# Two weight loads cut in two and issued between other casts, in a kernel of windowed attention and a ReGLU feed-forward layer

## The chip, the cores and the metric

The kernel runs on one core of one Trainium2 chip. The metric is the device time of one execution in microseconds, from the first to the last thing that the device does for it; the profile's span, from the first instruction to the last, is somewhat shorter. Times are medians of several executions.

The engines are named as in the profile: PE (matrix multiply; PEld is its weight load), DVE (vector), ACT (activation), POOL (general purpose) and SP (which here only issues transfers). Each takes its instructions in the order in which they stand in its queue; between engines there are semaphores. Transfers run on 16 DMA engines, which all issuing engines share.

## The reference

The inputs are q, k and v of 4 batches, 8 heads, 768 positions and 64 columns, and three weights. Attention is causal, with a window of 128 positions and 4 sink positions that are always seen; its output, 3072 tokens of 512, goes through a feed-forward layer of width 1536. Cut to what matters:

```python
scores = q @ k.T / 8                       # per batch and head
keep = (pos_k < 4) | ((0 <= pos_q - pos_k) & (pos_q - pos_k < 128))
a = softmax(where(keep, scores, -1e9))
x = (a @ v)                                # heads side by side: (3072, 512)
out = (maximum(x @ w_gate, 0) * (x @ w_val)) @ w_out
```

## The kernel before

The attention is cut into 16 **units**, each of two heads of one batch: unit 0 to 3 are batch 0, unit 4 to 7 batch 1, and so on. A unit's k, q and v are loaded as f32 into one of four staging buffers (`stg`), by SP, in the order k, q, then v in two halves, one per head. They are cast to bf16 into `kn`, `qn` and `vn`: for unit 0 by DVE and ACT in part, for all others by POOL (lines 126 and 129; line 130 repeats the four sink rows of v, line 338 casts a batch's last positions of v from `vt`). PE transposes `kn` and `qn` into `kT` and `qT` (line 149), computes the scores (line 181), ACT takes the exponential, DVE multiplies by the mask where that was not added to the scores, and PE multiplies by v and by ones for the sums (line 206). DVE normalises and leaves the unit's part of `xT` (lines 279 to 284).

The feed-forward layer is cut into **chunks** of 128 columns of the width 1536 and half a batch, 384 tokens: four matmuls against `w_gate` (line 294), four against `w_value` (line 300), ReLU on ACT, the product on DVE into `hT`. Its second product, with `w_out` (line 314), follows in pieces of up to three matmuls after each chunk. For batch 0 the chunks run over columns 0 to 383 for both halves of the tokens, six chunks, then over the next 384 columns, and so on. So the first **quarter** of a weight, 384 columns, serves chunks 0 to 5, and the second quarter is first wanted by chunk 6.

The order is written out by hand. The attention is a list of stages, and the table `PLAN` says how many of them are issued before which chunk: 28 before chunk 0. In these are all the stages of units 0 to 3 and the first three of unit 4. The transposes of unit 5 come after chunk 1. At one stage of unit x, `ahead(x)` issues work for later units: SP's loads, POOL's casts of unit x + 3, and POOL's loads of weights.

All weights are loaded by POOL, since these DMAs also cast from f32 to bf16: `load_w` for quarters of `w_gate` and `w_value`, `load_wo` for thirds of `w_out`. Their data goes over one queue, q0 in the profile; what SP issues goes over q1. Before the first stage POOL's order is: the casts of unit 1's k and q, unit 0's v, unit 1's v, unit 2's k and q; the first quarter of `w_gate`; the cast of unit 2's v. Then `ahead(0)` issues the first quarter of `w_value` and the casts of unit 3, and `ahead(1)` the casts of unit 4 and the second quarter of both weights. The casts of unit 5 follow in `ahead(2)`. Loads on SP stand in the order of units and run some units ahead; load k of unit 4 is issued at 15.56 us, its q at 16.42, its v at 17.41 and 18.03.

The functions that the change touches, and the lines that call them:

Of the kernel before, what the change touches and what calls it, by code (L numbers as in the profile page):

```python
# [33 lines left out]
def kernel(  # L34
# [12 lines left out]
    nc = tc.nc  # L47
# [4 lines left out]
    d_model, d_ff = moe_w_gate.shape  # L52
# [25 lines left out]
    wg = const.tile([128, KO, d_ff], BF16, name="wg")  # L78
    wv = const.tile([128, KO, d_ff], BF16, name="wv")
# [139 lines left out]
            nc.tensor.matmul(out=warm_ps[0][:, 0:128], lhsT=ident[:], rhs=ident[:], start=True, stop=True,  # L219
                             skip_group_check=True)  # L220

    def load_w(c, which=(1, 1)):

        n = d_ff // 4
        for w, dst, wanted in ((moe_w_gate, wg, which[0]), (moe_w_val, wv, which[1])):
            if wanted:
                nc.gpsimd.dma_start(out=dst[:, :, c * n:(c + 1) * n],
                                    in_=w.rearrange("(ko ki) n -> ki ko n", ki=128)[:, :, c * n:(c + 1) * n])

    def load_wo(c):  # L230
        nc.gpsimd.dma_start(out=wo[:, 4 * c:4 * c + 4, :],
                            in_=moe_w_out.rearrange("(ko ki) n -> ki ko n", ki=128)[:, 4 * c:4 * c + 4, :])
# [89 lines left out]
    with tc.manual_schedule():  # L322
        U = [Unit(i) for i in range(B * NP)]
        on_array = []

        def at(x):
            return U[x] if 0 <= x < len(U) else None

        def casts(u, what, eng=nc.gpsimd):
            for w in what:  # L330
                u.cast(w, eng)
# [5 lines left out]
        def cast_t(b):  # L337
            nc.gpsimd.tensor_copy(v6[b % 2][0:24, :, :], vt[b % 2][:])

        def load(x):  # L340
            if not U[x].p:
                load_t(U[x].b)
            for f in (lambda e: U[x].load_kq("k", e), lambda e: U[x].load_kq("q", e),
                      lambda e: U[x].load_v(e, 0), lambda e: U[x].load_v(e, 1)):
                f(nc.sync)

        def held(x):

            if x < len(U):
                nc.vector.memset(U[x].stg[0:1, 0:1], 0.0)  # L350
                load(x)
# [24 lines left out]
        cast_t(0)  # L376
        casts(U[1], "v")
        casts(U[2], "kq")
        load_w(0, (1, 0))
        casts(U[2], "v")  # L380
        load(4)

# [3 lines left out]
        def ahead(x):  # L386

            if x == 3:
                load(6)
            elif x == 4:  # L390
                load(7)
            elif x >= 5:
                held(x + 3)
            if 4 <= x < 6:
                for c in ((0,), (1, 2))[x - 4]:
                    load_wo(c)
            if x == 0:
                load_w(0, (0, 1))
            if at(x + 3) is not None:
                casts(at(x + 3), "kqv")  # L400
                if (x + 3) % NP == 0:
                    cast_t((x + 3) // NP)
            if x in (1, 3, 4):
                load_w((0, 1, 1, 2, 3)[x])
            if x == 0:
                load(5)

        def unit_stages(x):
            u, prev, nxt = U[x], at(x - 1), at(x + 1)

            def s(gi):
                def f():
                    if gi == 0 and nxt is not None and nxt.xbar:
                        nxt.X()
                    u.S(gi)
                    if x == 0 and gi < 2:
                        warm(5)
                return f

            def v():  # L420
                if prev is not None:
                    norm(prev, 1, ps_at if on_array else ps_gv)

            def t():
                if nxt is not None:
                    if not nxt.xbar:
                        nxt.T(not on_array)
                    nxt.sinkk()
                ahead(x)

            def v0():
                norm(u, 0, ps_at if on_array else ps_gv)

            if x < NP:
                return [s(0), s(1), v, t, s(2), v0]
            return [s(0), v, s(1), t, s(2), v0]

        def pair_stages(x):
# [26 lines left out]
            first_outs = outs(U[x - 1], 1) if x == 8 else outs(U[x - 1], 0, 1)  # L465
            a = then(scores((u, 0), (u, 1)))
            a_ = then(first_outs, lambda: ahead(x), w.sinkk)
            c = then(scores((u, 2), (w, 0)))
            d = then(outs(u, 0, 1), lambda: ahead(x + 1), lambda: nxt is not None and nxt.sinkk())
            e = scores((w, 1), (w, 2))  # L470
            first = [then(turn(w), a)] if w.xbar else [a, turn(w)]
# [28 lines left out]
        n = S // 2  # L500
        for ci, (b, h, m) in enumerate(ORDER):
# [11 lines left out]
            if count[b, h] == FM:  # L513
                for t in range(3 * h, 3 * h + 3):
                    w = d_model // 2 if (b, t) == (B - 1, 5) else d_model
# [38 lines left out]
```

## Time and profile before

| what | us |
|---|---|
| median of 4 runs (lowest, highest) | 257.73 (257.38, 257.97) |
| the profiled execution | 257.89 |
| its span, first to last instruction | 256.1 |
| PE busy | 247.7 |
| POOL busy | 62.1 |
| chain that ended last: PE's share of the span | 86% |
| the same: DMA's share | 8% |

Only the first 50 us have to do with the change. Of the stretch from 15 to 50 us, by fives (busy time of an engine in each, and the mean busy share of the 16 DMA engines):

| from | PE | DVE | ACT | POOL | DMA |
|---|---|---|---|---|---|
| 15 | 4.67 | 4.66 | 3.89 | 4.68 | 1.18 |
| 20 | 5.00 | 4.52 | 4.51 | 1.95 | 1.19 |
| 25 | 3.67 | 3.42 | 3.62 | 1.70 | 1.17 |
| 30 | 3.62 | 4.83 | 1.99 | 5.00 | 1.02 |
| 35 | 5.00 | 4.05 | 3.52 | 4.75 | 1.22 |
| 40 | 5.00 | 4.44 | 1.88 | 3.69 | 1.28 |
| 45 | 5.00 | 3.26 | 3.79 | 3.49 | 1.26 |

A DMA share above 1 means that packets' times overlap on an engine. Issuing a weight DMA keeps POOL for 0.74 to 0.88 us; a DMA's own time, to its landing, is told apart from that. The weight DMAs of the first quarter are issued at 15.04 (`w_gate`, landing 7.6 us later) and 17.52 (`w_value`, 10.3 us).

### The profile page before, as it was taken

The numbers are of one execution on the slowest core, as the hardware profiler recorded it, in microseconds if no ns is written. First come the engines' busy times: TensorE is split into PE (matmuls) and PEld (weight loads), VectorE is DVE, ScalarE is ACT, GpSimd is POOL, SyncE is SP. The second block draws the span as 40 slices with busy tenths as digits, with TensorE's granted clock in tenths as the row PEclk, the third lists the DMA queues.
The fourth block names the chain that finished last, engine by engine and source line by source line (L and its number), as shares of the span: only waits on it lengthen the run. The fifth ranks groups of instructions, "written<-read, shape, count | busy, mean of one in ns | idle before, by whom it ended". The sixth has DMA issues, their size and how long they took to land.

```text
span 256.1 us, 5232 instructions
## 1 busy us (share of the span) xinstructions
PE 247.7 (97%) x2058; PEld 144.6 (56%) x2058; DVE 148.7 (58%) x313; ACT 117.2 (46%) x190; POOL 62.1 (24%) x94
## 2 busy tenths in 40 slices
PE   7999699999999999999999999999999999999994
PEld 7556455556555565655565655656565555555443
DVE  2598788697956686787587654565575223223100
ACT  2878753736545426452635255152433332333212
POOL 6694597511705041404221300000000000000000
PEclk9999999999999999999999999999999999999999
DMA  7999999999668598859947712211011101111132
GB/s 207 306 269 259 288 242 255 202 252 220 118 129 160 116 176 170 126 109 180 221 109 146 144 41 72 35 41 44 0 41 44 41 0 41 44 41 41 44 123 84
DMA packets 73160, 33.17 MB, mean 130 GB/s; under 512 B 59696, under 2 KB 70192, under 8 KB 73136
## 3 DMA queue, kind: packets, MB, share of 16 engines
q1 hardware_dynamic: 65760, 27.73, 47.2%
q0 software_dynamic: 5808, 4.72, 11.6%
q10 hardware_dynamic: 1568, 0.39, 0.7%
q8 instruction: 16, 0.26, 0.4%
q14 instruction: 8, 0.07, 0.1%
HBM read 28.51 MB, written 6.29 MB: 136 GB/s over the span
## 4 chain that ended last, share of the span: by engine, by line
PE 86%; DMA 8%; DVE 2%; POOL 1%; issue 1%; ACT 0%; DVEq 0%; POOLq 0%; ACTq 0%
PE gp L294 26%; PE op L314 24%; PE vp L300 24%; PE ops L206 7%; PE sps L181 4%; DMA stg<-in_q_dram 4%; DMA vt<-in_v_dram 3%; DMA stg<-in_k_dram 1%; PE tkq L149 1%; POOL qn L126 1%; DVE ee L187 0%; DVE R L282 0%; DVE xT L284 0%; DVE R L279 0%; POOL vn L129 0%
## 5 line engine op out<-in xcount | busy, mean ns | idle before, releaser
L297 ACT ACTIVATE gs<-gp 128x384 f32<-128x384 f32 x96 | 47.4, 493 | 87.3 <-PE gp L294 56.4
L302 DVE TENSOR_TENSOR hT<-gs,vp 128x384 bf16<-128x384 f32 x96 | 52.0, 549 | 49.2 <-PE vp L300 46.9
L300 PE MATMUL vp<-xT,wv 128*128 128x384 bf16 x384 | 78.1, 326 | 1.0 <-DVE R L279 0.9
L294 PE MATMUL gp<-xT,wg 128*128 128x384 bf16 x384 | 78.5, 327 | 0.5 <-DVE xT L284 0.5
L314 PE MATMUL op<-wo,hT 128*128 128x512 bf16 (+1 forms) x300 | 74.4, 371 | 0.0
L300 PEld LDWEIGHTS <-wv 128*128 128x128 bf16 x384 | 37.5, 98 | 26.2 <-issue 1.5
L185 ACT ACTIVATE ee<-sps 128x1006 bf16<-128x1006 f32 (+2 forms) x48 | 44.6, 962 | 16.7 <-PE sps L181 16.4
L294 PEld LDWEIGHTS <-wg 128*128 128x128 bf16 x384 | 34.3, 98 | 29.8 <-issue 3.7
L314 PEld LDWEIGHTS <-hT 128*128 128x128 bf16 x300 | 29.4, 98 | 25.1
L187 DVE TENSOR_TENSOR ee<-ee,msk 128x1006 bf16<-128x1006 bf16 (+2 forms) x36 | 27.9, 776 | 18.3 <-ACT ee L185 18.0
L126 POOL CAST kn<-stg 128x768 bf16<-128x768 f32 x15 | 12.7, 850 | 56.3 <-DVE hT L302 29.8
L318 ACT COPY ot<-op 128x512 f32<-128x512 f32 (+1 forms) x25 | 14.2, 569 | 22.0 <-PE op L314 21.7
L282 DVE STREAM_TRANSPOSE R<-rc 128x384 f32<-128x384 f32 x32 | 18.5, 578 | 1.1
L284 DVE TENSOR_TENSOR xT<-ops,R 128x384 bf16<-128x384 f32 x32 | 17.8, 557 | 1.7
L279 DVE STREAM_TRANSPOSE R<-ops 128x384 f32<-128x384 f32 x24 | 13.9, 579 | 7.9 <-PE ops L206 7.6
L129 POOL CAST vn<-stg 128x768 bf16<-128x768 f32 x16 | 14.0, 875 | 13.7 <-DMA stg<-in_v_dram 9.3
L206 PEld LDWEIGHTS <-ones 128*64 128x64 bf16 x288 | 12.3, 110 | 7.2 <-issue 7.0
L206 PE MATMUL ops<-ee,vn 128*64 128x255 bf16 (+7 forms) x256 | 15.2, 240 | 0.0
L126 POOL CAST qn<-stg 128x768 bf16<-128x768 f32 x15 | 12.5, 831 | 10.6 <-DMA stg<-in_q_dram 10.6
L181 PEld LDWEIGHTS <-kT 64*128 64x128 bf16 x128 | 6.0, 93 | 13.5 <-issue 10.5
L181 PE MATMUL sps<-qT,kT 64*128 64x251 bf16 (+2 forms) x128 | 13.5, 250 | 0.0
L181 PE MATMUL sps<-qT,kTs 64*128 64x248 bf16 (+1 forms) x96 | 11.7, 253 | 0.5 <-DVE kTs L162 0.5
(57 smaller groups left out, 139.6 us busy)
## 6 DMA issues: line engine op xcount, KB each, us to landing
stg<-in_k_dram SPq DMA_DIRECT2D x16, 384.0 KB, 6.6
stg<-in_q_dram SPq DMA_DIRECT2D x16, 384.0 KB, 6.7
out_dram<-ot SPq DMA_DIRECT2D x23, 256.0 KB, 2.0
stg<-in_v_dram SPq DMA_DIRECT2D x30, 192.0 KB, 5.6
wg<-in_moe_w_gate_dram POOLq DMA_DIRECT2D x4, 384.0 KB, 7.2
wv<-in_moe_w_val_dram POOLq DMA_DIRECT2D x4, 384.0 KB, 9.7
wo<-in_moe_w_out_dram POOLq DMA_DIRECT2D x3, 512.0 KB, 12.4
stg<-in_v_dram ACTq DMA_DIRECT2D x2, 192.0 KB, 6.3
```

Of the source, the lines that this page charges most:

```text
L126: cp((self.kn if what == "k" else self.qn)[:], self.staging(what).rearrange("p h (n d) -> p n h d", d=64))
L181: nc.tensor.matmul(out=ps[:, h, c:c + w], lhsT=self.kw(j, r), rhs=qT[s][r, qa:qa + w], start=not self.biased, stop=True, skip_group_check= ...
L185: nc.scalar.activation(x, ps[:, :, 0:c], Act.Exp, bias=0.0, scale=scale)
L187: nc.vector.tensor_tensor(x, x, bc(msk[:, m0:m0 + c], 2), op=Alu.mult)
L206: nc.tensor.matmul(out=ps[1 - what][64 * h:64 * h + 64, qa - q0:qa - q0 + w], lhsT=self.vw(j, h) if what else ones[:], rhs=ee[s][:, gi, h, ...
L282: nc.vector.transpose(r[:, 1, 0:w], bass.AP(a.tensor, a.offset, [a.ap[0], [1, nb], [0, 32]]))
L284: nc.vector.tensor_tensor(xTs[u.b][:, u.p, c0:c0 + w], o[:, 0:w], r[:, 1, 0:w], op=Alu.mult)
L294: nc.tensor.matmul(out=gp[:, 0:n], lhsT=wg[:, ko, m * 128:(m + 1) * 128], rhs=x[:, ko, c0:c0 + n], start=ko == 0, stop=ko == KO - 1)
L297: nc.scalar.activation(gs[:, 0:n], gp[:, 0:n], Act.Relu, bias=0.0, scale=1.0)
L300: nc.tensor.matmul(out=vp[:, 0:n], lhsT=wv[:, ko, m * 128:(m + 1) * 128], rhs=x[:, ko, c0:c0 + n], start=ko == 0, stop=ko == KO - 1)
L302: nc.vector.tensor_tensor(hT[:, m, c0:c0 + n], gs[:, 0:n], vp[:, 0:n], op=Alu.mult)
L314: nc.tensor.matmul(out=op, lhsT=hTs[b][:, m, t * 128:(t + 1) * 128], rhs=wo[:, m, c0:c0 + n], start=m == 0, stop=m == FM - 1)
```

## The change

`load_w` takes the weights that it is to load as letters and a range of blocks of 128 columns within the quarter; without these it loads a whole quarter of both, as before. The first quarter of each weight is now loaded in two parts. The first part, columns 0 to 127, is issued for `w_gate` and then `w_value` between the q cast and the v cast of unit 2 (the third pair of heads). The second part, columns 128 to 383, is issued in `ahead(0)` in turn with the casts of unit 3 (the fourth pair): its k cast, `w_gate`, its q cast, `w_value`, its v cast. So POOL issues 13 weight DMAs in place of 11; the bytes are the same. Each of the new DMAs still has 512 rows to move, one of each of 128 partitions and 4 blocks, of 128 or 256 columns in place of 384. All other loads, and the work of all other engines, stand in the order in which they stood.

```diff
-    def load_w(c, which=(1, 1)):
-
-        n = d_ff // 4
-        for w, dst, wanted in ((moe_w_gate, wg, which[0]), (moe_w_val, wv, which[1])):
-            if wanted:
-                nc.gpsimd.dma_start(out=dst[:, :, c * n:(c + 1) * n],
-                                    in_=w.rearrange("(ko ki) n -> ki ko n", ki=128)[:, :, c * n:(c + 1) * n])
+    def load_w(c, which="gv", m=(0, 3)):
+
+        for x in which:
+            w, dst = (moe_w_gate, wg) if x == "g" else (moe_w_val, wv)
+            a, b = c * 384 + m[0] * 128, c * 384 + m[1] * 128
+            nc.gpsimd.dma_start(out=dst[:, :, a:b], in_=w.rearrange("(ko ki) n -> ki ko n", ki=128)[:, :, a:b])
...
         casts(U[1], "v")
         casts(U[2], "kq")
-        load_w(0, (1, 0))
+        load_w(0, m=(0, 1))
         casts(U[2], "v")
...
             if x == 0:
-                load_w(0, (0, 1))
+                casts(U[3], "k")
+                load_w(0, "g", (1, 3))
+                casts(U[3], "q")
+                load_w(0, "v", (1, 3))
+                casts(U[3], "v")
+            elif at(x + 3) is not None:
+                casts(at(x + 3), "kqv")
             if at(x + 3) is not None:
-                casts(at(x + 3), "kqv")
                 if (x + 3) % NP == 0:
                     cast_t((x + 3) // NP)
```

## The prediction

> **What bounds the kernel now.** I read the busy rows first: PE is busy 97% of the 256.1 us span, so only time that PE loses can be won, and PE cannot absorb a new wait. Then the chain of waits, from 16 us on (start, duration, what; lines left out between):
>
> ```profile
> 16.42 9.17 DMA stg<-in_q_dram
> ...
> 25.71 0.84 POOL qn L126
> ...
> 26.60 0.51 PE tq L149 x6
> ...
> 33.65 0.81 PE vp L300 x4
> 34.46 0.67 PE tkq L149 x12
> ...
> 42.77 0.65 PE vp L300 x4
> ```
>
> The end hangs on unit 4's q load: issued at 16.42, landed at 16.42 + 9.17 = 25.59, cast by POOL, transposed by PE. PE waits 1.3 us for that cast ("PE tq L149 <- POOL qn L126" among its waits); from 33.65 the chain is PE without a break. The change works on POOL and its DMA queue, so POOL's timeline is next (start, duration, instruction, in brackets the idle time before it):
>
> ```profile
> 23.08 0.82 POOL L126 CAST kn<-stg 128x768 bf16<-128x768 f32 x1 [1.89 <-DMA stg<-in_k_dram]
> 25.71 0.83 POOL L126 CAST qn<-stg 128x768 bf16<-128x768 f32 x1 [1.81 <-DMA stg<-in_q_dram]
> 29.07 0.83 POOL L129 CAST vn<-stg 128x768 bf16<-128x768 f32 x1 [2.52 <-DMA stg<-in_v_dram]
> 29.96 0.50 POOL L130 COPY vn<-vn 4x384 bf16<-4x384 bf16 x1
> 30.41 0.61 POOL L338 CAST v<-vt 24x512 bf16<-24x512 f32 x1
> 30.97 0.74 POOL L227 DMA_DIRECT2D wg<-in_moe_w_gate_dram  x1
> 31.71 0.75 POOL L227 DMA_DIRECT2D wv<-in_moe_w_val_dram  x1
> 32.44 0.84 POOL L126 CAST kn<-stg 128x768 bf16<-128x768 f32 x1
> 33.21 0.84 POOL L126 CAST qn<-stg 128x768 bf16<-128x768 f32 x1
> ```
>
> Unit 4's k, q and v casts each wait for a load. Behind the v cast stand the issues of the second quarter of w_gate and w_value, and unit 5's casts. That second quarter lands 10.8 us after 31.71, at 42.5, and the weight loads show who waits:
>
> ```profile
> 42.54 0.49 PEld L300 LDWEIGHTS <-wv 128*128 128x128 bf16 x4 [0.16 <-DMA wv<-in_moe_w_val_dram]
> ```
>
> The weight load waited for w_value and started 0.06 us before its matmul's turn at 42.60. So there is **no slack here**: PE can gain nothing past 42.6 unless this DMA lands earlier, and whatever it lands later than about 42.55 is lost, since PE takes instructions in order and is full afterwards.
>
> **What the DMA engines charge.** Packets and share of 16 engines by queue; stretches 44 to 45 (weights alone), 47.2 to 47.8 (w_out alone), 38 to 39 (weights with k and q), 24 to 24.5 (weights with v) and 41.2 to 41.7 (v nearly alone):
>
> ```profile
> q0 software_dynamic: 274, 0.20, 132.0%
> ...
> q0 software_dynamic: 119, 0.12, 118.7%
> ...
> q0 software_dynamic: 124, 0.09, 59.6%
> q1 hardware_dynamic: 126, 0.18, 59.2%
> ...
> q0 software_dynamic: 87, 0.07, 85.3%
> q1 hardware_dynamic: 82, 0.02, 33.5%
> ...
> q1 hardware_dynamic: 468, 0.12, 109.8%
> q0 software_dynamic: 18, 0.01, 16.7%
> ```
>
> Q0 carries weights, q1 what SP issues. Where both have work they move packets one for one (124 and 126, 87 and 82), whatever their size. Service times per engine: weights alone 16 x 1000/274, about 60 ns with the tiny semaphore packets taken off; k and q 16 x 1000/125 - 60 = 68; v about (16 x 500 - 18 x 60)/468 = 15. A weight and a v packet together take 16 x 500/85 = 94, so mixing costs 94 - 60 - 15, about 18. Each weight DMA is 512 packets, 32 per engine, of 1536 B read and 768 B written.
>
> **The change part by part.**
>
> *POOL.* Two more issues, 2 x 0.75 = 1.5 us. The issue of w_value before unit 2's v cast moves that from 16.18 to about 16.7; unit 3's k cast stays at about 18.1, its q cast goes from 19.02 to 19.6 (ends 20.4, PE reads it at 20.53), its v cast from 19.80 to 21.1. All is done by 22.5, before unit 4's k load lands (the cast starts at 23.08). Cost nothing, hidden by POOL's 1.89 us of idleness; without that cover, unit 4's k cast would be late, but PE takes it only at 24.84. No SP load's staging buffer is released late: the one of unit 6, held by unit 2's v cast, is issued at 28.0. POOL's later DMAs wait for older ones eight back; the last such pair is 7 us apart or more.
>
> *The first FFN chunk.* Its weights landed at 15.04 + 7.6 = 22.7 and 17.52 + 10.3 = 27.8 and are used at 29.9 and 30.9; nobody waited. Having 128 columns sooner is worth **0**. The parts for columns 128 to 383 are used from 32.6 on; issued at about 18.8 and 20.3 and given the 10.3 us of the slowest such row, they are there by 30.6.
>
> *Unit 4's k and q loads.* Per engine 16 packets each, one for one with weight packets. Now those are small: 512 B read, 256 written. If a packet has the fixed part that 15 ns at 256 B and 68 at 1536 give (a line of 0.041 ns per byte and 5 ns), it takes 5 + 55/3 = 23 ns instead of 60. 32 x 37 ns = 1.2 us at most, of which a part is lost because k and q packets only begin near 20 us, when part of the small ones has passed. Estimate: q lands 0.6 to 1.2 earlier, and most of PE's 1.3 us wait at 26.60 goes. That is what can be won, and it does not reach the end: what is late next is unit 4's **v**.
>
> *Unit 4's v load*, second half, issued at 18.03, landing 10.9 later, 28.9. By then all of the quarter has gone through the engines before (27.8), and will have after: v has 96 packets per engine, more than the 64 middle ones it alternates with. So v is late by the whole difference in DMA work: 64 packets at 60 = 3.84 us before; after, 64 at 23 + 64 at 5 + 55 x 2/3 = 42, 4.16 us: +0.3. And the quarter now alternates with v for some 64 packets an engine, where before w_value's last 25 or so did: I take 30 more x 18 ns = +0.5. Sum **+0.9 us** (rounded up for the second small part, which may start after the first is done and leave engines idle near 19.5). Bounds: no cost but for bytes, 0 (a little below if the last part is so late that v passes it); and packets by their recorded duration instead of their service time: 1.32 x 16000/274 = 77 ns at 768 B and 1.187 x 9600/119 = 96 at 1024 B, a line that gives 58 at 512 B and 39 at 256 B, so 64 x (58 + 39 - 77) = 1.3, with the mixing 1.8. I stay nearer the service times, since the engines overlap packets (shares above 100%).
>
> Two rules of the Trainium skill, DMA: Bandwidth & Descriptors, speak against the change. "Anatomy of one DMA" gives each software DMA a fixed 2.0 us; two more would be +4 us. The trace's row is the second quarter's two issues, 0.74 us apart, and what each DMA adds to a full queue is its packets' time; so I count none of it. "Why small descriptors are slow" puts about 3 cycles on each packet beside one per 32 B: 19, 35 and 51 cycles for 512, 1024 and 1536 B read, (19 + 35)/51 = +6% or +0.2 us, against +0.3 by this trace's row; the mixing, which that section does not have, is the larger term.
>
> *What hangs on v.* POOL's v cast from 29.07 to 30.0, the second quarter's issues from 30.97 to 31.9, unit 5's q cast ending at 34.05 + 0.9 = 34.95 where PE wanted it at 34.58: unit 5's transposes end 0.4 late though PE came early. Then w_value's second quarter lands at 42.5 + 0.9 = 43.4, and PE's matmul goes from 42.60 to 43.45: **+0.85 us**, carried to the end. The profiled execution took 257.89 us (256.1 of span), 0.16 over the median; 257.89 + 0.85 = 258.74, against the median 258.6.
>
> **The rivals.** (a) *Packets cost their bytes alone.* V is late by 0 to 0.3; the gain at 26.60 is taken back at 34.58 and 42.54. Against it: the 94 ns row. Time 257.5 to 258.2, no change. (b) *Faster:* q lands 1.2 us earlier and the last part starts so late that v's packets pass it; the second quarter's issue moves forward with v. For it: the first quarter's w_value took 10.3 us where w_gate took 7.6, so software DMAs issued among casts may start late. It decides once v lands more than 0.5 earlier; PE's next bound is its own 1.3 us wait, so 256.5 to 257.2, say 257.1. (c) *Much slower:* packets at their recorded durations, v late by 1.8, and the same at 42.54: 257.7 + 1.75 = 259.5. That the change does not do what it says is excluded for the order of issues on POOL; its small parts may still be served later than issued, which is (b).
>
> **How the numbers follow.** A measurement tells 0.2%, 0.5 us, from no change. Forecast (late v by 0.5 to 1.4) 0.54, (c) 0.15, (a) 0.19, (b) 0.12. Nearly all of the forecast's case is above 0.5 us: slower 0.68, same 0.19, faster 0.13. Range 257.2 to 259.6 takes in (a) and most of (c); the forecast's own is 258.1 to 259.1.
>
> **What would show it.** Right: unit 4's q cast before 25.3, PE's wait at tq under 0.7; unit 4's v cast at 29.6 to 30.4; a wait of PE or its weight loads on w_value near 43; q0 packets by 1024 more. Wrong: the v cast at 29.1 or before, or the weight load at 42.5 without a wait.

## The result, and the profile after

The changed kernel took 258.46 us (median of 43 runs, 256.15 to 259.29), the kernel before 257.88 (64 runs on the same chip, 256.50 to 259.97). The ratio over all these runs is 1.0017, with a 95% interval of 1.0003 to 1.0030: slower by about 0.45 us (the two medians are 0.58 us apart). The change costs a little, less than the +0.85 us of the forecast's sum. Ratios here and below leave out executions more than 1.5% above the fastest of the same kernel, of which these two kernels had none. The two profiled executions are 0.97 us apart: 257.89 with a span of 256.1 before, 258.86 with a span of 257.1 after.

The chain of waits of the changed kernel, from 18.7 us on (start, duration, what):

```profile
18.74 0.21 SPq L119
...
19.00 9.71 DMA stg<-in_v_dram
...
28.87 1.23 POOL vn L129
...
31.17 0.73 POOL wg L227
31.91 11.49 DMA wv<-in_moe_w_val_dram
...
43.45 0.82 PE vp L299 x4
```

Before, the chain went through unit 4's q load and was PE alone from 33.65 us on. Now q is no longer in it: it runs through unit 4's **v** load, the v cast that waits for it, and the second quarter of `w_value`, whose issue stands behind that cast. It reaches PE at 43.45 us. Of POOL's timeline, the lines that answer to those shown of before:

```profile
23.20 0.82 POOL L126 CAST kn<-stg 128x768 bf16<-128x768 f32 x1 [0.85 <-DMA stg<-in_k_dram]
24.21 0.83 POOL L126 CAST qn<-stg 128x768 bf16<-128x768 f32 x1 [0.19 <-DMA stg<-in_q_dram]
28.87 1.23 POOL L129 CAST vn<-stg 128x768 bf16<-128x768 f32 x1 [3.83 <-DMA stg<-in_v_dram]
30.16 0.50 POOL L130 COPY vn<-vn 4x384 bf16<-4x384 bf16 x1
30.61 0.61 POOL L337 CAST v<-vt 24x512 bf16<-24x512 f32 x1
31.17 0.74 POOL L227 DMA_DIRECT2D wg<-in_moe_w_gate_dram  x1
31.91 0.75 POOL L227 DMA_DIRECT2D wv<-in_moe_w_val_dram  x1
32.64 0.84 POOL L126 CAST kn<-stg 128x768 bf16<-128x768 f32 x1
33.41 0.84 POOL L126 CAST qn<-stg 128x768 bf16<-128x768 f32 x1
```

Unit 4's q cast starts at 24.21 in place of 25.71, so the change does bring q forward. The v cast has hardly moved (28.87, before 29.07). POOL now idles 3.83 us between the two, and everything behind the v cast (two weight issues, unit 5's casts) is where it was. What PE makes of that, from its timeline (the bracket is the idle time before the instruction and who ended it):

```profile
33.54 0.51 PE L149 MATMUL tkq<-ident,kn 128*128 128x128 bf16 x6 [1.24 <-POOL kn L126]
34.31 0.51 PE L149 MATMUL tkq<-ident,qn 128*128 128x128 bf16 x6 [0.26 <-POOL qn L126]
43.45 0.82 PE L299 MATMUL vp<-xT,wv 128*128 128x384 bf16 x4 [0.94 <-DMA wv<-in_moe_w_val_dram]
```

The 1.25 us wait at unit 4's q is gone, and three others have taken its place. The account is easiest by where each FFN chunk starts, after minus before:

| first matmul of chunk | before | after | difference |
|---|---|---|---|
| 0 | 30.38 | 28.87 | -1.51 |
| 1 | 32.76 | 30.60 | -2.16 |
| 2 (behind unit 5's transposes) | 34.97 | 34.65 | -0.31 |
| 6 (first with the second quarter) | 41.94 | 41.68 | -0.26 |
| 7 | 44.17 | 45.03 | +0.85 |
| 21 and all later | 70.83 | 71.78 | +0.95 |

PE wins 2.16 us, gives 1.85 back while it waits for unit 5's k and q casts, and 1.11 more at `w_value`. From chunk 7 on PE is full, and the difference is carried to the end, with 0.10 more at chunk 21. These are two single executions; how much the first one stands for the kernel before is taken up below.

### The profile page after: what moved, and what is told of

Same layout as the page of the kernel before. It is cut to its first block, busy times and chain, and to the rows that moved or that the text cites. A ratio compares the mean times of both kernels' runs of the same rounds, so it can differ in the third digit from the quotient of the medians.

```text
span 257.1 us, 5234 instructions
## 1 busy us (share of the span) xinstructions
PE 247.9 (96%) x2058; PEld 143.9 (56%) x2058; DVE 147.3 (57%) x313; ACT 117.0 (46%) x190; POOL 63.8 (25%) x96
## 3 DMA queue, kind: packets, MB, share of 16 engines
q0 software_dynamic: 6864, 4.72, 12.4%
HBM read 28.51 MB, written 6.29 MB: 135 GB/s over the span
## 4 chain that ended last, share of the span: by engine, by line
PE 82%; DMA 11%; SPq 3%; POOL 2%; issue 1%; ACT 0%; POOLq 0%; ACTq 0%
PE op L313 24%; PE gp L293 24%; PE vp L299 23%; PE ops L206 7%; DMA stg<-in_v_dram 7%; DMA wv<-in_moe_w_val_dram 4%; PE sps L181 3%; SPq L114 1%; SPq L334 1%; PE tkq L149 1%; POOL vn L129 1%; SPq L119 1%; POOL kn L126 0%; POOL wg L227 0%; POOL vn L130 0%
## 5 line engine op out<-in xcount | busy, mean ns | idle before, releaser
L299 PEld LDWEIGHTS <-wv 128*128 128x128 bf16 x384 | 37.5, 98 | 26.7 <-DMA wv<-in_moe_w_val_dram 1.3
L187 DVE TENSOR_TENSOR ee<-ee,msk 128x1006 bf16<-128x1006 bf16 (+2 forms) x36 | 26.9, 748 | 18.1 <-ACT ee L185 17.8
L281 DVE STREAM_TRANSPOSE R<-rc 128x384 f32<-128x384 f32 x32 | 18.5, 578 | 1.1
L206 PE MATMUL ops<-ee,ones 128*64 128x255 bf16 (+8 forms) x216 | 11.9, 236 | 0.0
```

Of the source, the lines that this page charges most:

```text
L187: nc.vector.tensor_tensor(x, x, bc(msk[:, m0:m0 + c], 2), op=Alu.mult)
L206: nc.tensor.matmul(out=ps[1 - what][64 * h:64 * h + 64, qa - q0:qa - q0 + w], lhsT=self.vw(j, h) if what else ones[:], rhs=ee[s][:, gi, h, ...
L281: nc.vector.transpose(r[:, 1, 0:w], bass.AP(a.tensor, a.offset, [a.ap[0], [1, nb], [0, 32]]))
L299: nc.tensor.matmul(out=vp[:, 0:n], lhsT=wv[:, ko, m * 128:(m + 1) * 128], rhs=x[:, ko, c0:c0 + n], start=ko == 0, stop=ko == KO - 1)
```

## The experiments

Numbers are the ratio to the kernel before on the same chip, with its 95% interval; single times and waits are of the profiled execution.

### Is it the second quarter's place behind the v cast?

In the kernel before and in the changed one, the second quarter (`load_w(1)`) is moved between unit 4's q and v casts:

```diff
-                casts(at(x + 3), "kqv")
+                casts(at(x + 3), "kq")
+                if x == 1:
+                    load_w(1)
+                casts(at(x + 3), "v")
...
-            if x in (1, 3, 4):
+            if x in (3, 4):
```

In the kernel before:

> The kernel before, with the second quarter of both weights issued between unit 4's q and v casts instead of behind the v cast. Theory A (the landing of w_value's second quarter sets the end in the kernel before too, at 42.54): the DMAs are issued at about 26.5 instead of 31.0 and land 2 to 4 us earlier, the weight load's wait is gone; but PE itself was only 0.06 us from its turn, so the end moves by no more than 0.5 us either way, unless unit 4's q load alone lets PE come earlier. Theory B (extra DMA work delays everything after it, the landing is not special): unit 5's k and q land later and the kernel is slower by 0.5 us or more.

In the changed kernel:

> The changed kernel with the same edit. Theory A: PE's wait of 0.9 us for w_value at 43.4 goes, unit 5's casts come about 1.2 us earlier, and what the earlier q load wins reaches the end: 0.8 to 1.8 us below the changed kernel, 0.4 to 1.3 us (0.2 to 0.5%) below the kernel before. Theory B: the weight packets then delay unit 5's k and q loads, and it stays at or above the kernel before.

Measured: 1.0083 (1.0055 to 1.0111) in the kernel before, 0.9957 (0.9941 to 0.9973) in the changed one. The same edit costs 0.8% in the one and wins 0.4% in the other. POOL's timeline of the changed kernel with the edit:

```profile
25.13 0.74 POOL L227 DMA_DIRECT2D wg<-in_moe_w_gate_dram  x1
25.86 0.75 POOL L227 DMA_DIRECT2D wv<-in_moe_w_val_dram  x1
28.78 0.83 POOL L129 CAST vn<-stg 128x768 bf16<-128x768 f32 x1 [2.17 <-DMA stg<-in_v_dram]
...
31.01 0.82 POOL L126 CAST kn<-stg 128x768 bf16<-128x768 f32 x1
```

The v cast is as late as before, but the two issues fill the idle time ahead of it, and unit 5's k cast starts at 31.01 in place of 32.64. `w_value`'s second quarter lands at 35.93 in place of 43.40. Chunk 7 starts 1.6 us earlier than in the kernel before, in place of 0.85 later: **the lead was real, and was lost at those two places.** In the kernel before the same edit ran into something else. The mask multiplication on DVE in the changed kernel without the edit, then the same one in the kernel before with the edit:

```profile
28.74 0.68 DVE L187 TENSOR_TENSOR ee<-ee,msk 128x1006 bf16<-128x1006 bf16 x1
```

```profile
29.53 2.29 DVE L187 TENSOR_TENSOR ee<-ee,msk 128x1006 bf16<-128x1006 bf16 x1
```

Of the latter run, POOL's timeline and then PE's:

```profile
28.68 0.50 POOL L130 COPY vn<-vn 4x384 bf16<-4x384 bf16 x1
29.14 0.60 POOL L338 CAST v<-vt 24x512 bf16<-24x512 f32 x1
29.69 0.82 POOL L126 CAST kn<-stg 128x768 bf16<-128x768 f32 x1
30.46 0.82 POOL L126 CAST qn<-stg 128x768 bf16<-128x768 f32 x1
```

```profile
32.36 0.81 PE L300 MATMUL vp<-xT,wv 128*128 128x384 bf16 x4 [1.89 <-DVE R L279]
```

The mask multiplication stood beside POOL's casts, which followed each other without a gap, and took 2.29 us in place of 0.68. PE then waited 1.89 us for DVE's next result (`R`) at its first product with `w_value` (0.92 in the kernel before). This is not the whole of the 0.8%: another 0.54 us goes at chunk 21, behind a mask multiplication of 2.10 us at 66.35, and 8 of the 14 executions that count had a mean granted clock of 0.993, where most of the kernel before have 0.997 or more. So this run says little on the weights.

### The other direction: the second quarter later still

In the changed kernel, the second quarter is issued behind unit 5's k and q casts:

```diff
+            elif x == 2:
+                casts(U[5], "kq")
+                load_w(1)
+                casts(U[5], "v")
...
-            if x in (1, 3, 4):
+            if x in (3, 4):
```

> The changed kernel with the second quarter of both weights issued behind unit 5's k and q casts instead of ahead of them. It parts the two waits that stand behind unit 4's v cast: unit 5's casts come 1.5 us earlier (PE's waits of 1.24 and 0.26 us for them go), the quarter is issued 1.6 us later. Theory A (w_value's second quarter sets the end): PE's wait for it grows from 0.9 to about 2.5 to 4 us, and the kernel is 1.2 to 2 us slower than the changed one, 1.6 to 2.5 us (0.6 to 1%) slower than the kernel before. Theory C (unit 5's transposes set it): 0.5 to 1.5 us faster than the changed kernel.

Measured: 1.0020 (0.9999 to 1.0041), as the changed kernel itself. In the profile unit 5's casts come earlier and PE keeps 1.3 us of its lead up to chunk 6, but then one wait of PE's timeline has it all:

```profile
42.97 0.82 PE L299 MATMUL vp<-xT,wv 128*128 128x384 bf16 x4 [1.50 <-DMA wv<-in_moe_w_val_dram]
```

The DMA of `w_value`'s second quarter was issued at 33.48, 1.57 us later than in the changed kernel, and yet landed at 42.92, 0.48 earlier than there. Its landing thus doesn't follow its issue at a fixed distance. Removing the wait for unit 5's casts alone wins nothing: the DMA takes the lead in their place. Neither theory's size came: A wanted 0.6 to 1% more than the kernel before, C a gain on the changed kernel.

### What makes the second quarter's DMA take 11 us?

Units 6 and 7 are loaded by SP in the same stretch. Unit 7's loads of k, q and v are left out of both kernels (its attention is then computed from unit 3's data, so both outputs differ):

```diff
             elif x == 4:
-                load(7)
+                pass
```

> The changed kernel, with the loads of unit 7's k, q and v left out (1.15 MB over q1; its attention is computed from unit 3's data, so the output differs). These loads are issued at 31.8 to 37.1 us and share the DMA engines with the second quarter of the weights. Theory (w_value's second quarter is late because its packets and those of units 6 and 7 share the engines, not because it is issued late): it lands at 41 us or before in place of 43.40, PE's 0.94 us wait for it is gone, the first 128 columns' lead stays, and the ratio to the kernel before is 0.994 to 0.997. Rival (its landing follows its issue at some 11.5 us, whatever the traffic): it lands after 43, PE waits 0.7 or more, ratio 1.000 to 1.003.

> The same leaving out in the kernel before. PE hardly waits for this quarter there, so both theories expect PE to be full from 33.65 us on as it was: ratio 0.998 to 1.001. It is the base for the run without unit 7 in the changed kernel: by the theory that one is 0.3 to 0.6% below this one, by the rival 0.1 to 0.3% above it.

Measured: 0.9966 (0.9949 to 0.9983) for the changed kernel, 0.9977 (0.9959 to 0.9996) for the one before. All waits of PE for unit 5's casts and for weights, from 14 to 50 us of the changed kernel without unit 7 (in total, times, longest):

```profile
PE tkq L149 <- POOL qn L126: 0.7, 1, 0.7
PE tkq L149 <- POOL kn L126: 0.3, 1, 0.3
```

There is no wait for `w_value` any more. It landed at 41.75, issued at 31.50: 10.25 us in place of 11.49. The theory wanted 41 or before; it was right on the wait and the ratio, and too strong on the landing. The comparison between the two runs is weak: 0.11% in favour of the changed kernel, where 0.3 to 0.6% was expected, with intervals that overlap; and the kernel before without unit 7 came out just below its expected 0.998 to 1.001. What is clear is that the changed kernel gains from leaving unit 7 out: 0.9966 and 1.0017 have intervals that don't meet. That the DMA is shorter for it is not shown: with unit 7's loads in place the same DMA, issued at 31 to 34 us, took 9.1 to 11.5 us in six traces of this case, and 10.25 lies among these. So the question of the heading stays open. Unit 5's casts still take PE's lead here, and unit 7's loads, the first of which is issued at 31.8 in the changed kernel, are not the reason.

The second of these runs brought what a sum over one profile could not see. Its profile shows the kernel before in another execution, and up to 30 us nothing differs in its program:

```profile
22.77 0.82 POOL L126 CAST kn<-stg 128x768 bf16<-128x768 f32 x1 [1.75 <-DMA stg<-in_k_dram]
24.93 0.83 POOL L126 CAST qn<-stg 128x768 bf16<-128x768 f32 x1 [1.33 <-DMA stg<-in_q_dram]
27.64 0.83 POOL L129 CAST vn<-stg 128x768 bf16<-128x768 f32 x1 [1.89 <-DMA stg<-in_v_dram]
```

Unit 4's v cast starts **1.43 us earlier** than in the profile that the prediction was made from. Several of the experiments differ from their kernel only behind unit 4's q cast, so they are further executions of the same start. Taken together (issue and landings from the trace, us; without unit 7, where it has no landing of v, the cast's start less the 0.15 us of the others):

| first quarter | run | SP issues v, second half | unit 4's q lands | unit 4's v lands | chunk 0 starts |
|---|---|---|---|---|---|
| as before | before | 18.03 | 25.59 | 28.92 | 30.38 |
| as before | quarter early, before | 18.02 | 24.88 | 27.64 | 29.66 |
| as before | no unit 7, before | 17.86 | 24.80 | 27.49 | 29.59 |
| as before | v late, before (below) | 18.49 | 25.15 | 27.92 | 29.94 |
| changed | after | 19.00 | 24.09 | 28.72 | 28.87 |
| changed | quarter early, changed | 18.83 | 24.23 | 28.63 | 29.02 |
| changed | quarter late, changed | 18.95 | 24.13 | 28.67 | 28.91 |
| changed | no unit 7, changed | 18.64 | 23.92 | 28.39 | 28.87 |
| changed | v late, changed (below) | 17.75 | 23.26 | 27.91 | 28.44 |
| changed | the same again | 18.75 | 23.95 | 28.51 | 28.73 |

By the medians the change brings q 1.0 us forward and puts v **0.8 us back** (27.78 to 28.57). The one profile of before was its slowest start of four. Four and six traces are few, though, and the time of that slow start is the ordinary one: 257.89 us, with a median of 257.88 for its kernel, while the other three belong to executions 0.5 to 0.8 us quicker than the median of theirs. So the 0.8 is an indication and not a measured shift.

SP's issue of v comes later in five of the six lower rows, and the traces show at which instruction. It is the one ahead of unit 4's loads, the last positions of v of batch 1 (`vt`); before and after:

```profile
14.93 0.52 SPq L335 DMA_DIRECT2D vt<-in_v_dram  x1
```

```profile
15.22 1.43 SPq L334 DMA_DIRECT2D vt<-in_v_dram  x1
```

It keeps SP 0.51 to 0.52 us in three of the four upper rows (1.07 in the fourth), 1.36 to 1.48 in five of the lower six, and 0.52 in the sixth. Unit 4's k and q are behind it too: q is issued at 17.57 after, 16.42 before, and lands 1.50 us earlier all the same.

### Everything out of the way of the lead

In the changed kernel the second quarter goes behind unit 4's q cast, and unit 4's v cast, for whose load POOL idles, behind unit 5's k and q casts:

```diff
+            elif x == 1:
+                casts(U[4], "kq")
+                load_w(1)
+            elif x == 2:
+                casts(U[5], "kq")
+                casts(U[4], "v")
+                cast_t(1)
+                casts(U[5], "v")
...
-            if x in (1, 3, 4):
+            if x in (3, 4):
```

> The changed kernel with the second quarter issued behind unit 4's q cast, and unit 4's v cast and its batch's last positions behind unit 5's k and q casts, which then wait for no v load. If DVE's multiplication by the mask at 28.9 is stretched by POOL's casts beside it (0.68 us in the changed kernel, where POOL stood still for it, 1.26 and 2.29 where POOL was casting), it takes about 0.7 again, the first w_value matmuls start 0.5 us earlier, and the kernel is at or 0.2 to 0.7 us below the one with the quarter moved alone: 0.4 to 0.8% below the kernel before. If the stretch has another cause: the same as that one within 0.3 us.

Measured: 255.58 us, 0.9920 (0.9893 to 0.9948): faster than both kernels, by 2.1 us against the one before. It was run again on another chip, beside the same edit in the kernel before, to see whether the split has a part in it:

> The changed kernel with the second quarter behind unit 4's q cast and unit 4's v cast behind unit 5's k and q casts, a second time and on the chip of the runs beside it: 0.990 to 0.994 by the theory; above 0.996 the first run's gain was chance.

> The kernel before, with the second quarter behind unit 4's q cast and unit 4's v cast behind unit 5's k and q casts; the first quarter whole in its old places. Theory (the split brings unit 4's q some 1.4 us earlier, which is kept once the second quarter and the v cast are out of the way): without the split only the later losses go, unit 4's q lands at 25.6 as before, ratio 0.996 to 1.000, so 0.4 to 0.8% above the changed kernel with the same edit (0.992). Rival (the split does nothing, the moved quarter does all): 0.990 to 0.994.

Measured: 255.62 us, 0.9932 (0.9908 to 0.9957) in the changed kernel; 257.50 us, 1.0001 (0.9978 to 1.0025) in the one before. PE's waits from 14 to 50 us of the first of these two:

```profile
PE gp L293 <- DVE xT L283: 0.4, 1, 0.4
PE vp L299 <- DVE R L278: 0.3, 1, 0.3
PE tq L149 <- POOL qn L126: 0.2, 1, 0.2
```

None of them is for a weight or for unit 5. In its profile chunk 1 starts 2.30 us earlier than in the kernel before and every chunk from 4 on 2.44: nothing is given back. Of the two profiles with the split, one had SP's issue of v 1.00 us earlier than the other (17.75 and 18.75), and the medians are the same to 0.04 us. The same edit without the split is worth nothing, so the split is needed for it; and the split without the edit costs 0.17%.

### Parts of the change alone

**The small DMAs without the move.** In the kernel before, each first quarter is cut into 128 and 256 columns, both issued one behind the other in the quarter's old place (with the changed kernel's `load_w`):

```diff
-        load_w(0, (1, 0))
+        load_w(0, "g", (0, 1))
+        load_w(0, "g", (1, 3))
...
-                load_w(0, (0, 1))
+                load_w(0, "v", (0, 1))
+                load_w(0, "v", (1, 3))
```

> The kernel before with each weight's first quarter cut into columns 0 to 127 and 128 to 383, both parts issued back to back where the whole was. It has the small packets and the two more issues, not the new places. If the small packets' DMA work is what costs (my sum gave 0.3 us for the packets and 0.5 for mixing): slower by 0.3 to 0.9 us. If the places on POOL matter and not the packets: within 0.3 us of the kernel before.

Measured: 1.0027 (1.0008 to 1.0046). Unit 4's q lands at 25.19, within the spread of before, and its v at 28.66, as late as in the changed kernel. So cutting alone, without a gain for q, has a cost and no return. What the cost is made of is not parted here: SP issued that half of v late in this run too (18.90).

**The move without the cut.** The whole first quarter of `w_gate` behind unit 3's k cast, that of `w_value` behind its q cast (again with the changed `load_w`):

```diff
-        load_w(0, (1, 0))
...
             if x == 0:
-                load_w(0, (0, 1))
+                casts(U[3], "k")
+                load_w(0, "g")
+                casts(U[3], "q")
+                load_w(0, "v")
+                casts(U[3], "v")
```

> The kernel before with the first quarters whole, w_gate issued behind unit 3's k cast (18.1 instead of 15.0) and w_value behind its q cast (19.6 instead of 17.5), where the changed kernel issues its second parts. It has the new places, not the small packets. Unit 4's q lands 1 us or more earlier, w_value's first quarter lands near 29 to 30, just in time for 30.9. If the end hangs on w_value's second quarter alone: within 0.4 us of the kernel before. If small packets were the cost of the change: faster than the kernel before by 0.3 us or more.

Measured: 1.0001 (0.9975 to 1.0026). Q lands earlier still, at 23.24, but `w_value`'s first quarter lands at 32.29 (29 to 30 was expected), and PE's only large wait from 14 to 50 us takes the gain:

```profile
PE vp L299 <- DMA wv<-in_moe_w_val_dram: 2.4, 1, 2.4
```

**The whole first quarter early.** Both weights between unit 2's q and v casts, in the kernel before:

```diff
-        load_w(0, (1, 0))
+        load_w(0)
...
             if x == 0:
-                load_w(0, (0, 1))
```

> The kernel before with both first quarters whole, w_gate and then w_value, between unit 2's q and v casts. No small packets, and nothing of the weights left for the v load to mix with late. If DMA work is only shared out one packet for one: unit 4's q lands as late as in the kernel before or later (25.5 to 26.5), its v 0 to 0.5 us earlier, and the end stays within 0.5 us of the kernel before. If the place of w_value behind the v cast matters for itself (its packets began 4 us after the issue, w_gate's 2.7): slower or faster by more than that.

Measured: 0.9997 (0.9968 to 1.0026). The ratio is a mean over two groups. Of the 22 executions 13 took 256.4 to 257.2 us with a mean granted clock of 0.997 or more, which is below the median of the kernel before (257.68); the other nine took 259.4 to 261.2 with 0.987 to 0.993, and the ratio leaves out three of these. The profile is of one of the nine (259.77): PE waits 1.74 us for unit 4's q in it, the opposite of the run before it, and the clock falls, as shown at the end. The quicker 13 have no profile, so what parts the groups is open, and so is whether the uncut quarter can be had early without the fall. For the late place one wait takes what another wins; for the early place the even ratio doesn't say that.

**The second quarter ahead of unit 4's k cast,** in the changed kernel:

```diff
+            if x == 0:
+                load_w(1)
```

(behind unit 3's casts, with the second quarter no longer issued at `x == 1`)

> The changed kernel with the second quarter issued still earlier, behind unit 3's v cast and ahead of unit 4's k cast. w_value's second quarter is then never waited for; but its packets run beside unit 4's v and unit 5's k and q loads, which land 2 to 4 us later. Theory A alone (only that landing matters) would give the same time as with the quarter behind unit 4's q cast. If one-for-one sharing of packets is right, unit 5's transposes wait instead: 0.5 to 2 us slower than that one.

Measured: 1.0010 (0.9981 to 1.0039). The quarter now shares the engines with unit 4's q, and PE waits again: 0.5 us for q casts up to unit 4's, 0.6 for unit 5's, 0.8 for DVE. That profile is of an execution of 257.56 us. The ratio flatters this kernel: it leaves out nine of the 22 executions, and the median of all 22 is 259.99 us, against 257.68 before; 12 of them had a mean granted clock of 0.993 or less. So too early is at least as bad as too late, and it is the place between unit 4's q and v casts, where POOL idled, that wins.

## Why the prediction was right, and where it was not

The direction was right: slower, with the loss where the sum had it, at `w_value`'s second quarter. That the sum's 43.4 and 43.45 for its landing and its matmul agree with the trace's 43.40 and 43.45 is luck, since the way there was another (below). The size was +0.85 in the sum and +0.97 between the profiled executions, but +0.45 by the ratio of many runs, which is the better measure. That is about half of the sum, and a little under the 0.5 us that the prediction took as the least to be told from no change; it is told here by 107 runs. The median, 258.46 against 258.6, looks closer than the size was, since the kernel before came out at 257.88 in place of 257.73. Step by step:

- **Unit 4's q, 0.6 to 1.2 us earlier:** right. It was 1.50 earlier than in the profile of before, 1.0 by the medians of the table. PE's wait for it went from 1.25 us to nothing.
- **The first FFN chunk gains nothing from having its weights sooner:** right; the parts landed by 28.2 and nobody waited. But the run with the whole quarter late shows why the first 128 columns have to come early once the rest is late: 2.44 us of PE.
- **POOL's two more issues at no cost:** right. All of it was done by 22.35, and unit 4's k cast began at 23.20.
- **The price of the small packets, 23 and 42 ns:** right. Of the changed kernel's queues, 18.0 to 18.5 and 24.9 to 25.4 us:

```profile
q0 software_dynamic: 335, 0.08, 170.4%
...
q0 software_dynamic: 184, 0.09, 137.2%
```

  Q0 has these stretches nearly to itself, and 16 x 500/335 is 24 ns for 256 B written; 16 x 500/184 is 43 for 512 B. Each packet's own duration is longer than that (the share is far above 100%), which was the upper bound's error. q0 has 6864 packets in place of 5808: 1024 for the data, 32 small ones.
- **Unit 4's v, 0.9 us late, and with it the v cast at 29.6 to 30.4:** this is the step that failed as it was put. The v cast came at 28.87, and the prediction named 29.1 or before as the sign that it is wrong. Against the profile of before, v landed 0.20 us *earlier*. Against the three other executions of the same start (27.49 to 27.92) it is 0.8 to 1.2 late, near the 0.9 of the sum. The base was one execution whose v was 1.0 to 1.4 later than in those three, and nothing in the prediction allowed for such a spread.
- **The cause given for the late v (0.3 for packets, 0.5 for their mixing):** not borne out. The sum has all of v's packets held up by the quarter's, and most were not. Of the 1536 data packets of unit 4's v, 1400 had begun by 24.6 us after and by 26.7 before (packets of 256 B on q1 from 20.3 us on, counted in the traces; 23.2 to 24.6 in the six executions of the changed start, 25.6 to 26.7 in the four of before), although SP issued that half up to 1 us later. At 21.5 to 22.5 us alone 623 of them went, when q0 moved 59: the second parts' first packets came only 3 us after their issue. This is what rival (b) described, that v's packets pass the last part. But the landing waits for the last packets: from the 1400th to the landing it took 1.8 to 2.2 us before and 4.1 to 4.9 in the changed start. Why the last ones lag is open. Part may be SP's later issue, a queue that the sum took as unmoved: in the sixth execution, with the issue at 17.75, v landed at 27.91, within the spread of before. Why SP takes longer for `vt` is open as well: it does so too in the run with the whole quarter late, where POOL issues no DMA at that time. (In the sum itself, 94 - 60 - 15 is 19 and not 18, which changes nothing.)
- **Unit 5's transposes 0.4 us late:** they ended 0.31 early (34.31 + 0.51 = 34.82, before 34.46 + 0.67 = 35.13), since the v cast and all that stands behind it came earlier than the sum had them. The wait was there, 1.24 + 0.26 us, and was the first of the two places where the lead went.
- **W_value's second quarter +0.9:** right in size, by luck. Its issue was only 0.20 later (31.91; the v cast took 1.23 in place of 0.83 us, beside DVE's mask multiplication). Its DMA took 11.49 in place of 10.79. The sum had it issued 0.9 later and carried that 10.8 over unchanged, so two errors cancelled.

Of the rivals, "packets cost their bytes alone" has the packets' rows against it, by a little (24 and 43 ns, where a third and two thirds of 60 are 20 and 40); its time, up to 0.5 us above the kernel before, holds the measured +0.45 as well as the forecast does, so the time alone doesn't decide between the two. "Much slower" is excluded by the time, 258.46 where it wanted 259.5. "Faster" was nearer than its chance says: the lead of 1 us or more that it needs is there, and a move of two issues and one cast turns it into 0.7 to 0.8%. What it got wrong is that v's landing, and with it the second quarter, would come forward with v's packets.

## What to carry to other kernels

A load that lands earlier wins only as far as the next instruction on the casting engine that still waits: look at what stands behind that wait (here two weight issues and the next unit's casts behind a v cast that idled 3.83 us), and move it ahead together with the gain. Before working out a change of 1 us from one profile, ask how much the same landing moves between executions of the same program; here it was 1.4 us over four executions, more than the effect. A part that costs 0.2% alone can be what a larger gain needs, so a change with an early win and a late loss is worth a second edit before it is dropped.

## What the runs showed of the hardware

**DVE and POOL hold each other up.** The mask multiplication of 128 x 1006 bf16 elements took 0.68 us in the changed kernel and 2.29 beside POOL's casts. The excess of 1.61 us is what the two casts that began after it take (0.82 + 0.82). In the two profiles with the quarter early and v late, where no cast stood beside it, it took 0.68. The other way round, POOL's v cast at 28.87, which began while the multiplication of 28.74 to 29.42 ran, took 1.23 in place of 0.83. The Trainium skill, "SBUF — State Buffer", section "SBUF: two separate sides", has the two engines share a pair of ports that one of them holds for a whole instruction, while the other is blocked; it counts a vector instruction with two inputs in SBUF, beside a GpSimd one that reads SBUF, among the cases. Both durations come within 0.15 us of that: the multiplication would have waited for the end of the second cast (31.28) and run its 0.68 us to 31.96, where it ended at 31.82; the v cast would have waited 0.55 us for the end of the multiplication, and was 0.40 longer. So a shift of less than a microsecond in POOL's order decided on 1.6 us of DVE, for which PE then waited.

**The clock fell although PE was not idle throughout.** In the profile of the run with the whole first quarter early, the windows show (us, length, busy PE, PEld, DVE, ACT and POOL, granted clock, DMA share, GB/s):

```profile
25.00:28.00 3.00, 1.26 (x16) 0.75 (x18) 2.08 (x4) 1.02 (x2) 0.83 (x1) 1.00 1.12 322
28.00:31.00 3.00, 3.00 (x39) 2.16 (x40) 1.59 (x4) 2.04 (x3) 2.87 (x5) 0.50 1.11 268
31.00:32.00 1.00, 1.00 (x19) 0.70 (x16) 0.91 (x2) 0.41 (x1) 1.00 (x2) 0.80 0.96 311
```

PE was busy for 1.26 of 3 us, between waits of 0.52 and 1.74 us, and then ran at half speed for 3.4 us (3 us at 0.50, and 0.4 of the next at half to make 0.80). So waits close together can cost more than their sum: half speed for 3.4 us takes 1.7 us of PE's work, and 0.5 x 3.4 / 258 is 0.7%, about what the mean granted clock of most of this kernel's nine longer executions lacks (0.993). How little PE must do for the clock to fall was not measured. In the changed kernel's profile the granted clock stays at full speed.
